# Attention on one core: the end of phi on VectorE, row sums through PSUM, M_prev's products in four pieces, a new order

## The chip, the cores and the metric

The kernel runs on one NeuronCore of a Trainium2 chip. Its engines are TensorE (PE; its weight loads are PEld), VectorE (DVE), ScalarE (ACT), GpSimd (POOL) and SyncE (SP, which here issues loads and stores). The metric is the device time of one execution in microseconds (us); less is better. Beside the times there is the profile of one execution.

## The reference

Three stages run one after the other. The change touches the first; the other two follow from its output. Of the attention stage, for each of 4 batches and 8 heads (576 tokens of 64 values):

```python
scores = scale * np.matmul(q, k.transpose(0, 1, 3, 2))
scores = np.where(causal, -1000000000.0, scores)
scores = scores - scores.max(-1, keepdims=True)
a = np.exp(scores)
a /= a.sum(-1, keepdims=True) + 1e-09
local = np.matmul(a, v)
def phi(x):
    return np.where(x > 0, x, np.exp(x) - 1.0) + 1.0
q_p = phi(q)
mem_ret = np.einsum('bhsd,bhde->bhse', q_p, M_prev)
mem_norm = np.einsum('bhsd,bhd->bhs', q_p, z_prev)[..., None] + 1e-06
g = 1.0 / (1.0 + np.exp(-beta))[None, :, None, None]
return g * (mem_ret / mem_norm) + (1 - g) * local
```

Then a mixture of experts takes each of the 2304 tokens (512 values) to one of 8 experts, picked by the largest of `x @ w_gate`, through two weight matrices with a ReLU between, and scales by the gate's probability. Last, an MLP (512 to 2048 to 512, with an ELU) works on all tokens.

## The kernel before

The attention stage goes over 16 *pairs*: a batch `b` and two neighbouring heads, pair `p = 4 b + hp`. For each pair, q and k are turned (transposed) on PE (`L92`) and copied out of PSUM into `ab`, k by DVE (`L596`) and q by ACT (`L593`). There are five blocks of scores, `i` = 3, 4, 2, 1, 0 in the code's list; block `i` < 4 holds 128 query rows and 128 (i+1) keys of both heads, block 4 the last 64 rows. Each block is a product on PE (`L639`, `L643` for the mask; `L650`, `L653` for block 4), a minimum over the row on DVE (`L661`; the scores are held negated), and an exponential on ACT (`L666`), which also sums the row into `st`. PE turns the weights (`L92` again, tile `a`), ACT or DVE copies them out (`L524` on ACT, `L527` on DVE, into `aA` for blocks 0 to 2 and `aB` for 3 and 4), and PE multiplies them with v (`L741`). The result is copied to `xT` by ACT (`L524`), and `L536` with `iw` brings it back to tokens together with the gate's logits. DVE scales it by the reciprocal row sums (`L773`, tile `ls`).

phi(q) is min(exp(q), 1) + relu(q): ACT makes both terms (`L606`, `L610`), POOL takes the minimum and adds (`L621`, `L622`, tiles `ex` and `qpT`). `L536` with `mb` multiplies it by M_prev, with w_gate already multiplied in (below), and DVE scales that (`L717`, `L721`, `L725`, tile `ms`). POOL adds `ms` and `ls` into the rows of the batch (`L785`, three adds a pair; DVE does it for the last pair).

The row sums sit in `st`, 12 to 20. Block 4's need the other half of the partitions, so PE moves them (`L739` with `swap`, into column 1000 of the PSUM tile of `L741`), DVE copies that back (`L748`), adds 1e-9 and multiplies by 1 - g (`L752`), and takes the reciprocal (`L756`).

Before pair 0, `constants` multiplies M_prev by w_gate: PE turns M_prev by halves (`L351`, four pieces), ACT copies them (`L355`), PE multiplies (`L364`, one piece for each half, 16 products each; `L365` brings z_prev), DVE copies into `mb` (`L369`, `L370`). After every fourth pair, `gate_plan` picks the experts of the batch's tokens on DVE (`L820` to `L862`), makes five pairs of one-hot tables (`L870`, `L873`, then `L885`), and PE multiplies these (`L892`). The gate of batch 3 lies in the next stage. At the end of the attention stage `first_parts` turns (`L1141`) and splits (`L1155`, `L1158`, `L1161`, tiles `x`) the first tile of tokens for the experts.

All four PSUM rings of this stage are one: four tiles of two banks (`pat`), handed out in the order of the plan.

What sets the order is a planner. Each step is an operation with an engine (or several to choose from), a cost in ns, and the keys that it reads and writes. `Plan.order` places them one by one: it takes the engine that can start soonest, and on it the step of least `prio` among those that can start within `slack` (`sa` in `KNOBS`) of the first. `off` holds the offsets of `prio`, `es` the engines that a copy may choose from. The instructions are issued in the planned order, so each engine runs its list front to back and waits at its head.

Of the kernel before, what the change touches and what calls it, by code (L numbers as in the profile page):

```python
# [94 lines left out]
class Plan:  # L95
# [169 lines left out]
def constants(tc, ctx, c, M_prev, z_prev, beta, w_gate):  # L265
# [78 lines left out]
    for h in range(2):  # L344
        for n in range(2):
            def mk(h, n):
                bk = Slot(c.rs)

                def f():
                    for x in range(8):  # L350
                        nc.tensor.transpose(bk.t[0:D, x * D:(x + 1) * D], c.mb[hss[h], 8 * n + x, 0:D], c.ident[hss[h], hss[h]])  # L351
                pl.op("PE", 450, f, r=["mld"], w=[bk], prio=K["mem"] - 30)

                def f():
                    nc.scalar.copy(mT[:, h, 8 * n:8 * n + 8, :].rearrange("p x d -> p (x d)"), bk.t[0:D, 0:512])  # L355
                pl.op("ACT", ca(512), f, r=[bk], w=[("mT", h, n)], prio=K["mem"] - 30)
            mk(h, n)
    for h in range(2):
        def mk(h):
            bq = Slot(c.rs)  # L360

            def f():
                for x in range(NPAIR):
                    nc.tensor.matmul(bq.t[hss[h], x * E:(x + 1) * E], mT[:, h, x, :], wg[:, 2 * (x % (H // 2)) + h, :], start=True, stop=True)  # L364
                nc.tensor.matmul(bq.t[hss[h], 256:256 + B * H], zr, c.ident[0:B * H, 0:B * H], start=True, stop=True)  # L365
            pl.op("PE", 900, f, r=["mld", ("mT", h, 0), ("mT", h, 1), ("raw", 0, 0), ("raw", 0, 1)], w=[bq], prio=K["mem"] - 20, dense=0.15)

            def f():
                nc.vector.tensor_copy(c.mb[hss[h], :, D:XB], bq.t[hss[h], 0:NPAIR * E].rearrange("p (x e) -> p x e", e=E))  # L369
                nc.vector.tensor_copy(c.mb[hss[h], :, XB:MW].rearrange("p x o -> p (x o)"),  # L370
                                      bq.t[hss[h], 256:256 + B * H].rearrange("p (x h) -> p x h", h=2)[:, :, h])
            pl.op("DVE", 400, f, r=[bq], w=["mb"], prio=K["mem"] - 20)
        mk(h)
# [100 lines left out]
def cps(n):  # L474
    return 330 + 0.83 * n
# [6 lines left out]
def attention(tc, ctx, c, q, k, v, M_prev):  # L482
# [55 lines left out]
    def pair(p):  # L538
# [80 lines left out]
        def f():  # L619
# [3 lines left out]
        pl.op("POOL", cps(S) + cpt(S), f, r=[se], w=[sqT, (se, "phi")], prio=at("phi"))  # L623
# [6 lines left out]
        def scores(i, ps):  # L630
# [23 lines left out]
            pl.op("PE", n / 0.6 + 90 if i < 4 else 1000, f if i < 4 else f4, r=fk, w=[s, (sa[i], "own"), (ss, "own", i)], prio=ps + O["S"], mode=1 if i < 4 else 3)  # L654
# [7 lines left out]
            pl.op("DVE", cv(2 * nn), f, r=[s], w=[(ss, "n", i)], prio=ps + O["min"])  # L662
            for h in range(2 if i < 4 else 1):
                def mk(h):
                    def f():
                        nc.scalar.activation(sa[i].t[:, h, :] if i < 4 else sa[4].t[:, 0:S].rearrange("p (y n) -> p y n", y=2), src()[:, h, :] if i < 4 else src(), AF.Exp,  # L666
                                             bias=ss.t[:, 2 * i + h:2 * i + h + 1], scale=-1.0, accum_out=ss.t[:, 12 + 2 * i + h:13 + 2 * i + h])
                    pl.op("ACT", ca(nn if i < 4 else S, acc=True), f, r=[s, (ss, "n", i)], w=[(sa[i], h), (ss, "s", i, h)], prio=ps + O["exp"] + K["hd"] * h)
                mk(h)

        def weights(i, ps):
# [10 lines left out]
            pl.op("PE", nb * 2 * TURN, f, r=[(sa[i], h) for h in range(2 if i < 4 else 1)], w=[w, (so, "own", i)], prio=ps + O["T"], mode=1)  # L682
# [9 lines left out]
            evac(f"T{i}", nb * P, dst, src, r=[w], w=[(so, i)], prio=ps + O["Te"])  # L692

        for o, i in enumerate(ORD):
            scores(i, pr + K["step"] * o)
        for o, i in enumerate(ORD):
            weights(i, pr + K["step"] * o)
# [33 lines left out]
        for g, (so, tiles, n, n0) in enumerate(((sA, (0, 1, 2), 384, P), (sB, (3, 4), 192, 512))):  # L731
            for j in range(tiles[-1] + 1):
                def mm(g, so, tiles, n, n0, j):
# [8 lines left out]
                    pl.op("PE", (n - o) / 0.6 + (60 if first else 5), f, r=[svi] + [(so, i) for i in tiles if j <= i] + ([(ss, "s", 4, 0), "swap"] if first else []),  # L742
                          w=[wx, (sx, "own", g, j)], prio=at("av") + g, mode=2)
# [66 lines left out]
def gate_plan(tc, c, b, lg, xrow, rl, rx, ring, pr):  # L810
# [4 lines left out]
    def bc(x):  # L815
# [4 lines left out]
        (330, lambda: v.tensor_reduce(G.L, lg.t.rearrange("p i c e -> p i e c"), axis=AX.X, op=ALU.add)),  # L820
# [47 lines left out]
    def table(i):  # L868
# [5 lines left out]
        pl.op("DVE", 160, f, r=[("rq", b)], w=[("rone", i)], prio=pr)  # L874
        pl.op("DVE", 170, f2, r=[("rq", b)], w=[("qone", i)], prio=pr)
# [10 lines left out]
    pl.op("DVE", 240, f, r=[("rone", i) for i in range(NI)], w=["rrow"], prio=pr)  # L886
# [839 lines left out]
```

## Time and profile before

| | |
|---|---|
| median of 3 runs | 940.1 us (939.83 to 941.58) |
| the profiled execution | 943.06 us |
| its span, first to last instruction | 941.3 us |
| mean granted TensorE clock | 0.988 of full speed |
| attention stage | to 231.5 us, where the experts' first product starts |

The profiled execution's time is 1.8 us above its span, and 3.0 us above the median. The stages of the experts and of the MLP take the other 710 us.

### The profile page before, as it was taken

Reading aid. Unit: us, or ns where it says so; the run is one execution under the profiler, and the core shown is the slowest. Engines: PE = TensorE matmul, PEld = TensorE weight load, DVE = VectorE, ACT = ScalarE, POOL = GpSimd, SP = SyncE. Lnnn points to the kernel's source line nnn. Section 1 sums busy time; section 2 is a strip of 40 time slices with the busy share of each in tenths; the row PEclk is TensorE's granted clock in tenths of the full one; section 3 lists DMA queues with packets and bytes.
Section 4 is the critical chain, followed back from the end, with each engine's and each line's share of the span. In section 5 each row is a group of like instructions: output and inputs, shape, how many; then the busy total and the mean of one; then the engine's idle time right before and its main releaser. Section 6 shows DMA issues by size and latency. Waiting matters only on the chain. (4 is left out here: it accounts for less than half of the span.)

```text
span 941.3 us, 19282 instructions
## 1 busy us (share of the span) xinstructions
PE 906.4 (96%) x7334; PEld 743.4 (79%) x7334; DVE 606.9 (64%) x1104; ACT 447.7 (48%) x879; POOL 174.7 (19%) x208
## 2 busy tenths in 40 slices
PE   9998989988999999999999899999999999999996
PEld 6676767766788888888878789988888888888895
DVE  2768686866864579548887785555565556555553
ACT  3887878876553467347676561221222122212311
POOL 2443434433101222221211100010001000100100
PEclk7999999999999999999999999999999999999998
DMA  6333343351814795589995550110011000100000
GB/s 113 83 87 103 78 128 71 82 189 59 319 35 158 256 353 194 177 280 365 329 344 194 172 184 1 34 45 1 1 46 46 1 23 12 46 1 1 23 23 23
DMA packets 97113, 110.07 MB, mean 117 GB/s; under 512 B 65391, under 2 KB 65391, under 8 KB 94705
## 3 DMA queue, kind: packets, MB, share of 16 engines
q1 hardware_dynamic: 90992, 95.26, 31.7%
q0 software_dynamic: 4800, 13.18, 3.9%
q8 instruction: 59, 0.97, 0.4%
q10 hardware_dynamic: 1216, 0.30, 0.2%
q14 instruction: 46, 0.37, 0.1%
HBM read 87.94 MB, written 23.41 MB: 118 GB/s over the span
## 5 line engine op out<-in xcount | busy, mean ns | idle before, releaser
L1535 ACT ACTIVATE elu<-pt 128x512 f32<-128x512 f32 x72 | 43.0, 598 | 266.0 <-PE pt L1527 264.0
L1560 PE MATMUL pt<-w,gh 128*128 128x512 f32 x432 | 134.2, 392 | 0.5 <-DVE gh L1439 0.5
L1327 PE MATMUL pm<-w,hh 128*128 128x512 f32 x368 | 125.1, 401 | 0.8 <-ACT y L1340 0.8
L1543 DVE TENSOR_SCALAR elu<-elu 128x512 f32<-128x512 f32 x72 | 30.8, 428 | 126.3 <-ACT elu L1535 126.3
L661 DVE TENSOR_REDUCE st<-pat 128x2 f32<-128x256 f32 (+4 forms) x80 | 62.6, 793 | 50.1 <-PE pat L643 47.9
L1560 PEld LDWEIGHTS pt<-w,gh 128*128 128x128 f32 x432 | 79.6, 188 | 16.4 <-DVE gh L1439 0.9
L666 ACT ACTIVATE a<-pat,st 128x128 f32<-128x128 f32 (+2 forms) x144 | 78.0, 547 | 25.9 <-DVE st L661 25.0
L1560 PE MATMUL pt<-w,gl 128*128 128x512 f32 x216 | 84.2, 390 | 0.0
L1327 PEld LDWEIGHTS pm<-w,hh 128*128 128x128 f32 x368 | 69.2, 188 | 14.5 <-ACT y L1340 1.2
L1327 PE MATMUL pm<-w,hl 128*128 128x512 f32 x184 | 71.9, 391 | 0.3 <-DVE hl L1161 0.3
L1527 PE MATMUL pt<-yTh,w 128*128 128x256 f32 (+1 forms) x288 | 69.2, 319 | 0.0
L639 PE MATMUL pat<-ab 64*128 64x128 f32 (+3 forms) x256 | 50.5, 492 | 7.2 <-DVE st L661 7.0
L1547 DVE SCALAR_TENSOR_TENSOR tnh<-tnh,elu 128x512 f32<-128x512 f32 x72 | 49.7, 691 | 8.4 <-ACT tnh L1539 2.4
L1284 PE MATMUL pm<-w,x 128*128 128x512 f32 x216 | 51.8, 392 | 1.2 <-DVE w L1161 0.9
L1442 DVE TENSOR_TENSOR gl<-tnh,gh 128x512 fp32r<-128x512 f32 x72 | 49.7, 691 | 4.5 <-DVE gh L1439 0.5
L1527 PEld LDWEIGHTS pt<-yTh,w 128*128 128x128 f32 x288 | 49.2, 190 | 3.9
L1551 DVE SCALAR_TENSOR_TENSOR tnh<-pt,tnh 128x512 f32<-128x512 f32 x72 | 49.6, 691 | 3.3
L1284 PEld LDWEIGHTS pm<-w,x 128*128 128x128 f32 x216 | 40.2, 188 | 10.1 <-DVE w L1161 1.4
L1161 DVE TENSOR_TENSOR hl<-pm,hh 128x512 fp32r<-128x512 f32 x46 | 31.4, 685 | 25.5 <-ACTq L1258 14.4
L1560 PEld LDWEIGHTS pt<-w,gl 128*128 128x128 f32 x216 | 40.5, 188 | 9.0 <-DVE gl L1442 0.4
L621 POOL TENSOR_SCALAR ex<-ex 128x576 f32<-128x576 f32 x16 | 34.2, 2135 | 68.2 <-ACT ex L606 68.2
L1527 PE MATMUL pt<-yTl,w 128*128 128x256 f32 (+1 forms) x144 | 45.8, 318 | 0.0
(335 smaller groups left out, 2038.5 us busy)
## 6 DMA issues: line engine op xcount, KB each, us to landing
wraw<-in_moe_w_dram SPq DMA_DIRECT2D x24, 1024.0 KB
wrbw<-in_moe_w_dram SPq DMA_DIRECT2D x12, 1024.0 KB
wide<-in_moe_w_in_dram SPq DMA_DIRECT2D x16, 512.0 KB
wf<-half SPq DMA_DIRECT2D x32, 256.0 KB
wide<-in_moe_w_out_dram SPq DMA_DIRECT2D x16, 512.0 KB
wide<-wf SPq DMA_DIRECT2D x9, 512.0 KB
v<-in_v_dram SPq DMA_DIRECT2D x32, 128.0 KB
wraw<-yd SPq DMA_DIRECT2D x14, 258.0 KB
```

The source lines that it names most:

```text
L621: nc.gpsimd.tensor_scalar(e, e, 1.0, 0.0, op0=ALU.min, op1=ALU.add)
L639: nc.tensor.matmul(s.t[:, 512 * h:512 * h + n], row(1)[hs, i * P:(i + 1) * P], row(0)[hs, 0:n], start=True, stop=False)
L661: nc.vector.tensor_reduce(ss.t[:, 2 * i:2 * i + (2 if i < 4 else 1)], src(), axis=AX.X if i < 4 else AX.XY, op=ALU.min)
L666: nc.scalar.activation(sa[i].t[:, h, :] if i < 4 else sa[4].t[:, 0:S].rearrange("p (y n) -> p y n", y=2), src()[:, h, :] if i < 4 else src ...
L1284: nc.tensor.matmul(g[hf].t, a.t[:, cc, :], b[:, 512 * hf:512 * (hf + 1)], start=(cc == 0 and n == 0), stop=(cc == 3 and n == 2))
L1327: nc.tensor.matmul(y.t, a.t[:, 2 * (q % 2) + jj, :], b[:, 512 * jj:512 * (jj + 1)], start=(q == 0 and jj == 0 and n == 0), stop=(q == 3 an ...
L1442: nc.vector.tensor_sub(lo(), src(), hi().bitcast(F32))
L1527: nc.tensor.matmul(h.t[:, n * j + n0:n * j + n1], w(cc, a, ft), b(cc), start=(cc == 0 and x == 0), stop=(cc == 3 and x == 2))
L1535: nc.scalar.activation(se.t, h.t, AF.Exp)
L1547: nc.vector.scalar_tensor_tensor(st.t, st.t, 0.0, se.t, op0=ALU.min, op1=ALU.mult)
L1551: nc.vector.scalar_tensor_tensor(st.t, h.t, 0.0, st.t, op0=ALU.max, op1=ALU.add)
L1560: nc.tensor.matmul(acc[a].t, y.t[:, n * j + P * a:n * j + P * (a + 1)], wsub(1, k, ft // 2)[:, ft % 2, :], start=(ft == 0 and x == 0), sto ...
```

## The change

- **phi.** The minimum and the addition become one DVE instruction (`fv`, L622 of the new file); the planner's table allows DVE alone (`qe`).
- **Row sums.** PE brings all ten columns of row sums into PSUM (nine through the identity, the tenth through `swap`), and DVE's addition and multiplication read them there; the copy is gone.
- **M_prev.** PE turns it in two pieces that use both halves of the array, ACT copies two tiles of twice the width, and the products are four pieces, each over both halves. DVE copies both halves at once.
- **The gate's costs** in the planner are raised (650 for 330, 195 for 160, 205 for 170, 300 for 240).
- **The table of the order** is new: an offset for each block in place of one step between blocks, other engines to choose from.

```diff
-    "m_g": -500, "wq": 0.64, "sa": 57.1, "sm": 50.0, "s2": 0.0, "step": -26642.3, "hd": -1515.1, "mem": 417833.9, "xg": 4,
+    "m_g": -500, "wq": 0.64, "sa": 70.4, "sm": 50.0, "s2": 0.0, "hd": 270570.9, "mem": -170390.9, "xg": 4,
...
+    for n in range(2):
+        def mk(n):
+            bk = Slot(c.rs)
 
             def f():
+                for x in range(8):
+                    for h in range(2):
+                        turn(nc, bk.t[0:D, 512 * h + x * D:512 * h + (x + 1) * D], c.mb[hss[h], 8 * n + x, 0:D], c.ident, h)
+            pl.op("PE", 16 * TURN, f, r=["mld"], w=[bk], prio=K["mem"] - 30, mode=1, dense=0.25)
...
+    bq = Slot(c.rs)
+    for n in range(4):
+        def mk(n):
+            def f():
+                for x in range(4 * n, 4 * n + 4):
+                    for h in range(2):
+                        nc.tensor.matmul(bq.t[hss[h], x * E:(x + 1) * E], mT[:, h, x, :], wg[:, 2 * (x % (H // 2)) + h, :], start=True, stop=True)
...
-        def f():
+        def fv():
+            nc.vector.scalar_tensor_tensor(sqT.t[:, 0:S], se.t[:, 0:S], 1.0, sqT.t[:, 0:S], op0=ALU.min, op1=ALU.add)
+
+        def fp():
             e = se.t[:, 0:S]
-            nc.gpsimd.tensor_scalar(e, e, 1.0, 0.0, op0=ALU.min, op1=ALU.add)
+            nc.gpsimd.tensor_scalar(e, e, 1.0, None, op0=ALU.min)
...
-                            nc.tensor.matmul(wx.t[h * D:(h + 1) * D, 1000:1001], c.swap[:, h * D:(h + 1) * D], ss.t[:, 20:21], start=True, stop=True)
+                            nc.tensor.matmul(wx.t[h * D:(h + 1) * D, 1000:1009], c.ident[:, h * D:(h + 1) * D], ss.t[:, 12:21], start=True, stop=True)
+                            nc.tensor.matmul(wx.t[h * D:(h + 1) * D, 1009:1010], c.swap[:, h * D:(h + 1) * D], ss.t[:, 20:21], start=True, stop=True)
...
-            nc.vector.tensor_copy(ss.t[:, 21:22], wx.t[:, 1000:1001])
+            nc.vector.scalar_tensor_tensor(ss.t[:, 12:22].rearrange("p (i h) -> p i h", h=2), wx.t[:, 1000:1010].rearrange("p (i h) -> p i h", h=2), 1.0e-9,
+                                           c.omg[:, h0:h0 + 2].unsqueeze(1).to_broadcast([P, NI, 2]), op0=ALU.add, op1=ALU.mult)
```

In the new file the lines are 2 to 8 higher: `L593` is now L595, `L661` L667, `L666` L672, `L596` L598, `L524` and `L527` L526 and L529, `L752` L755, `L773` L777, `L870` L874, `L873` L877. The lists of the expert and MLP stages hold the same instructions in the same order on every engine.

**The start, on ACT.** Before: four copies of M_prev's turned halves, then q of pair 0 (`ab`), phi's two terms and the first exponentials (`a`).

```order
L355 ACT_TABLE_LOAD
L355 COPY wraw_75<-pat_96 64x512
L355 COPY wraw_75<-pat_94 64x512
L355 COPY wraw_75<-pat_97 64x512
L355 COPY wraw_75<-pat_95 64x512
L593 ACTIVATE ab_198<-pat_97 128x576
L606 ACTIVATE ex<-pat_97 128x576
L610 ACTIVATE qpT_220<-pat_97 128x576
L666 ACTIVATE a_204,st_228<-pat_96,st_228 128x128 x2
```

Now, on the same engine, up to the first copies of turned weights (`aA`):

```order
L608 ACTIVATE ex<-pat_94 128x576
L612 ACTIVATE qpT_220<-pat_94 128x576
L672 ACTIVATE a_204,st_228<-pat_97,st_228 128x128 x2
L672 ACTIVATE a_206,st_228<-pat_96,st_228 128x256 x2
L355 COPY wraw_75<-pat_97 64x2x512
L355 COPY wraw_75<-pat_96 64x2x512
L672 ACTIVATE a_208,st_228<-pat_95,st_228 128x384 x2
L672 ACTIVATE a_210,st_228<-pat_94,st_228 128x512 x2
L672 ACTIVATE a_212,st_228<-pat_97,st_228 128x576
L336 ACTIVATE omg<-g 128x8
L337 ACTIVATE g<-g 128x8
L526 COPY aA_216<-pat_95 128x2x128
```

M_prev's copies moved from ahead of pair 0's first exponentials to between them, and the two steps that wait for beta (`L336`, `L337`) from behind two copies of weights to ahead of the first. On PE, M_prev's work moved in the same way: its products stood before the first scores, and now stand behind the scores of block 4. On SP, q and v of pair 0 are now issued ahead of M_prev, which came first; the 24 loads ahead of beta (`L325`) are the same 24.

**A gate, on DVE.** Before, between k's copy of pair 5 (`L596`) and its first minimum (`L661`), behind other steps of the gate:

```order
L596 TENSOR_SCALAR ab_198<-pat_96 128x576
L838 RECIPROCAL raw_69<-gsm_157 128x3
L907 TENSOR_REDUCE gcnt_155<-goh_154 128x8
L839 RECIPROCAL raw_70<-gsm_157 128x2
L856 TENSOR_TENSOR geq_152<-pat_97,ebase 128x40
L857 TENSOR_TENSOR geq_152<-geq_152,goh_154 128x40
L858 TENSOR_REDUCE gsl_158<-geq_152 128x5
L859 TENSOR_TENSOR gsli_159<-gsl_158,inval 128x5
```

Now `L856` (new L860) stands a pair later, among the last steps of pair 5; the tables follow it, and end ahead of pair 6's phi (L622) and first minimum:

```order
L727 RECIPROCAL rn_233<-rn_233 128x10
L860 TENSOR_TENSOR geq_152<-pat_97,ebase 128x40
L731 TENSOR_TENSOR ms_235<-pat_95,rn_233 128x2x5x72
L861 TENSOR_TENSOR geq_152<-geq_152,goh_154 128x40
L862 TENSOR_REDUCE gsl_158<-geq_152 128x5
L863 TENSOR_TENSOR gsli_159<-gsl_158,inval 128x5
L864 TENSOR_SCALAR gsli_159<-gsli_159 128x5
L865 TENSOR_SCALAR gsli_159<-gsli_159 128x5
L866 CAST grq_160<-gsli_159 128x10
L529 COPY aB_219<-pat_95 128x2x5x64
L874 TENSOR_SCALAR raw_70<-col,grq_160 128x128
L877 TENSOR_SCALAR qone<-col,grq_160 128x144
```

So the gate's DVE work, which stood between two pairs in one piece, now stands in two pieces a pair apart.

**A plain pair, on ACT.** Pair 2's last exponentials and copies before:

```order
L666 ACTIVATE a_210,st_228<-pat_97,st_228 128x512 x2
L666 ACTIVATE a_212,st_228<-pat_95,st_228 128x576
L524 COPY aA_216<-pat_97 128x4x128
L524 COPY aA_216<-pat_96 128x6x128
L524 COPY aB_218<-pat_97 128x2x5x64
L524 COPY aB_218<-pat_94 128x8x128
```

Now:

```order
L672 ACTIVATE a_210,st_228<-pat_97,st_228 128x512 x2
L526 COPY aA_216<-pat_96 128x2x128
L672 ACTIVATE a_212,st_228<-pat_94,st_228 128x576
L526 COPY aA_216<-pat_97 128x4x128
L526 COPY aB_218<-pat_94 128x2x5x64
L526 COPY aB_218<-pat_95 128x8x128
```

Block 0's small copy came from DVE to ACT, ahead of block 4's exponential; block 2's copy (128x6x128) went to DVE. In other pairs DVE takes block 1's or block 4's copy in its place. On PE, k of the next pair, which was turned between blocks 2 and 4, is now turned behind block 3.

## Rows read from the trace of the kernel before

**Rows 1.** The page, part 1: busy time, share of the span, instructions.

```profile
PE 906.4 (96%) x7334; PEld 743.4 (79%) x7334; DVE 606.9 (64%) x1104; ACT 447.7 (48%) x879; POOL 174.7 (19%) x208
```

**Rows 2.** Windows of a pair: length; busy PE, PEld, DVE, ACT, POOL; clock; DMA share; GB/s.

```profile
106.82:118.88 12.06, 11.85 (x230) 8.75 (x226) 7.91 (x14) 10.17 (x28) 5.53 (x5) 1.00 0.33 76
...
131.72:146.78 15.06, 12.74 (x252) 9.85 (x250) 12.44 (x31) 12.04 (x33) 5.54 (x5) 1.00 0.49 139
...
183.75:200.87 17.12, 14.56 (x259) 11.40 (x255) 13.77 (x41) 12.00 (x33) 5.54 (x5) 0.90 0.35 106
```

**Rows 3.** phi's exponential, once a pair: first and last start; pair 2's start.

```profile
L606 ACT ACTIVATE ex<-pat x16: 645/670/697, 13.7 to 214.1; 128x576 f32<-128x576 f32 x16
...
41.12 0.65 ACT L606 ACTIVATE ex<-pat 128x576 f32<-128x576 f32 x1
```

**Rows 4.** Waits of PE, 108.95 to 121.01 us (total, times, longest).

```profile
PE pat L92 <- ACT a L666: 0.2, 1, 0.2
```

**Rows 5.** Timeline of PE in a plain pair.

```profile
108.95 0.49 PE L639 MATMUL pat<-ab 64*128 64x128 f32 x4
...
118.03 1.51 PE L741 MATMUL pat<-aA,v 128*64 128x384 f32 x12
119.38 0.23 PE L739 MATMUL pat<-st,swap 128*64 128x1 f32 x4
```

**Rows 6.** Timeline of DVE in that pair.

```profile
109.63 0.42 DVE L661 TENSOR_REDUCE st<-pat 128x2 f32<-128x256 f32 x1 [3.97 <-PE pat L643]
...
110.16 1.07 DVE L752 SCALAR_TENSOR_TENSOR st<-st,omg 128x10 f32<-128x10 f32 x1
111.14 0.68 DVE L661 TENSOR_REDUCE st<-pat 128x2 f32<-128x512 f32 x1
```

**Rows 7.** Timeline of PE: M_prev's turns, pairs 0 and 1's first scores, pair 0's M_prev.

```profile
7.54 1.78 PE L351 MATMUL pat<-ident,mb 64*64 64x64 f32 x32
...
16.89 0.80 PE L639 MATMUL pat<-ab 64*128 64x128 f32 x4
...
22.94 0.83 PE L536 MATMUL pat<-mb,qpT 64*64 64x73 f32 x36
...
30.67 0.49 PE L639 MATMUL pat<-ab 64*128 64x128 f32 x4
```

**Rows 8.** Timeline of pair 0: beta's load, its first user, pair 1's phi.

```profile
18.84 0.60 SPq L325 DMA_DIRECT2D g<-in_beta_dram  x1
...
24.60 1.01 DVE L331 COPY iw<-ident 64x64 f32<-64x64 f32 x8
...
28.41 0.66 ACT L606 ACTIVATE ex<-pat 128x576 f32<-128x576 f32 x1
```

**Rows 9.** Timeline of DVE in the second gate.

```profile
134.69 1.49 DVE L873 TENSOR_SCALAR qone<-col,grq 128x144 bf16<-128x144 f32 x1
136.10 0.28 DVE L870 TENSOR_SCALAR raw<-col,grq 128x128 bf16<-128x128 f32 x1
...
136.50 0.28 DVE L870 TENSOR_SCALAR raw<-col,grq 128x128 bf16<-128x128 f32 x1
```

**Rows 10.** Timeline of DVE in pair 14, while POOL is idle.

```profile
205.18 0.17 DVE L752 SCALAR_TENSOR_TENSOR st<-st,omg 128x10 f32<-128x10 f32 x1
```

**Rows 11.** The page, part 5: a DVE instruction with two inputs from SBUF.

```profile
L1547 DVE SCALAR_TENSOR_TENSOR tnh<-tnh,elu 128x512 f32<-128x512 f32 x72 | 49.7, 691 | 8.4 <-ACT tnh L1539 2.4
```

**Rows 12.** Timeline of POOL in that pair.

```profile
109.80 1.40 POOL L622 TENSOR_TENSOR qpT<-ex,qpT 128x576 f32<-128x576 f32 x1
114.78 2.00 POOL L785 TENSOR_TENSOR raw<-ms,ls 128x80 f32<-128x80 f32 x3 [3.59 <-DVE ls L773]
```

**Rows 13.** Timeline of PE and DVE at the end of the stage.

```profile
222.69 0.72 PE L1141 MATMUL pat<-ident,ex 128*128 128x128 f32 x4 [0.36 <-DVE st L661]
...
224.87 0.68 DVE L1161 TENSOR_TENSOR x<-pat,x 128x512 fp32r<-128x512 f32 x1
...
231.51 1.20 PE L1284 MATMUL pm<-wq,x 128*128 128x512 f32 x4 [0.87 <-DVE ls L773]
```

More of the change, by code (lines that the diff above doesn't have):

```diff
@@ L244 @@
-    "es": {"x": ("ACT",), "T0": ("ACT", "DVE"), "T3": ("ACT", "DVE"), "k": ("DVE",), "T1": ("ACT",), "T4": ("ACT", "DVE"), "q": ("ACT",), "T2": ("ACT",)},
-    "wait": 25, "first": 34686.5, "stick": 1430924.2,
+    "nv": 2, "na": 2, "na4": 2, "nx": 2, "nls": 2, "wide": 1, "de": ("DVE", "POOL"), "busy": [0, 0, 0], "early": 120578.4, "late": 500, "mld": -2631.6,
+    "gate": 345828.7, "warm": [52, 0.0, 200.0], "qe": ("DVE",),
+    "off": {"tk": 898454.0, "tq": 882278.5, "hk": -760325.6, "hq": -759364.9, "px": 735151.8, "phi": 1087364.4, "S3": -529669.6, "S4": -1296033.8, "S2": -790035.1, "S1": -972813.3, "S0": -1302605.5, "min3": -50550.3, "min4": -410935.5, "min2": 719181.7, "min1": -45115.7, "min0": 332677.3, "exp3": 329358.7, "exp4": 631684.7, "exp2": -50550.0, "exp1": 518666.4, "exp0": 344677.0, "T3": 859665.0, "T4": 626578.9, "T2": 622423.5, "T1": 518666.8, "T0": 516520.2, "Te3": -47668.1, "Te4": 807182.8, "Te2": -1296012.9, "Te1": -509705.8, "Te0": -561958.2, "fin": -50955.8, "mm": 807201.2, "md": -1303158.8, "ms": 238704.4, "avA": -328031.8, "avB": -684654.8, "ave": -328185.5, "rw": -1410391.2, "ls": -829501.3, "add": -8135.8},
@@ L246 @@
+    "es": {"x": ("ACT",), "T0": ("ACT",), "T3": ("ACT",), "k": ("ACT", "DVE"), "T1": ("ACT", "DVE"), "T4": ("ACT", "DVE"), "q": ("ACT", "DVE"), "T2": ("ACT", "DVE")},
+    "wait": 25, "first": 1087370.1, "stick": 1227967.1,
 }
@@ L368, in f @@
             def f():
[L369 to L373, printed above, removed]
+                nc.scalar.copy(mT[:, :, 8 * n:8 * n + 8, :], bk.t[0:D].rearrange("p (h x d) -> p h x d", h=2, d=D))
@@ L374, in constants, with f @@
+    def f():
+        nc.vector.tensor_copy(c.mb[:, :, D:XB], bq.t[:, 0:NPAIR * E].rearrange("p (x e) -> p x e", e=E))
+        for h in range(2):
+            nc.vector.tensor_copy(c.mb[hss[h], :, XB:MW].rearrange("p x o -> p (x o)"),
+                                  bq.t[hss[h], 256:256 + B * H].rearrange("p (x h) -> p x h", h=2)[:, :, h])
+    pl.op("DVE", 400, f, r=[bq], w=["mb"], prio=K["mem"] - 20)
     routing_constants(tc, c)
@@ L681, in weights @@
             so = sA if i < 3 else sB
-            pl.op("PE", nb * 2 * TURN, f, r=[(sa[i], h) for h in range(2 if i < 4 else 1)], w=[w, (so, "own", i)], prio=ps + O["T"], mode=1)
+            pl.op("PE", nb * 2 * TURN, f, r=[(sa[i], h) for h in range(2 if i < 4 else 1)], w=[w, (so, "own", i)], prio=at(f"T{i}"), mode=1)
             def dst():
@@ L691, in src @@
                 return w.t.rearrange("p (z x) -> p z x", z=2)[:, :, 0:nb * D].rearrange("p z (y q) -> p z y q" if i == 4 else "p z (y q) -> p y z q", q=D)
[L692 to L697, printed above, removed]
+            evac(f"T{i}", nb * P, dst, src, r=[w], w=[(so, i)], prio=at(f"Te{i}"))
+        for i in ORD:
+            scores(i)
+        for i in ORD:
+            weights(i)
         sx, srn = Slot(r_xT), Slot(r_rn)
@@ L885, in f @@
         v.tensor_scalar(c.rrow, c.rone, c.row, None, op0=ALU.mult)
-    pl.op("DVE", 240, f, r=[("rone", i) for i in range(NI)], w=["rrow"], prio=pr)
+    pl.op("DVE", 300, f, r=[("rone", i) for i in range(NI)], w=["rrow"], prio=pr)
     def f():
```

58 lines of the change are left out of this document (20 added, 38 removed).

## The prediction

> **What bounds it now.** I read the engines' busy shares first: TensorE 96% [rows 1]. That share is a mean over three stages, and two of them (experts, MLP) hold the same instructions in the same order before and now, so I let them shift as a block. Everything is decided ahead of the experts' first product.
>
> In that stage I took the windows between one pair's first scores and the next's [rows 2]. A plain pair lasts 12.06 us with TensorE busy 11.85, ACT 10.17, DVE 7.91; the two with a gate last 15.06 and 17.12. How much all gates cost comes from phi's exponential, once a pair: from 41.12 (pair 2) to 214.1 (pair 15) are 13 intervals, 172.95 us [rows 3]; 13 plain ones would be 156.8. The excess is **16.2 us**, and it lies at the three gates, which are what can be won in the middle of the stage.
>
> In the wait view of a plain pair TensorE waits 0.2 us [rows 4], and its timeline runs from the first scores (108.95) to the products with v (118.03) without a hole that anything else could fill [rows 5]. So a plain pair is bound by the list on TensorE itself; ACT is next, with 1.9 us of room; DVE has a hole of 3.97 us ahead of its first minimum [rows 6]. POOL works 5.53 of 12.06 and nobody on the path waits for it. The start is the other place to look at: pair 0's first scores come at 16.89 only, behind M_prev's work [rows 7].
>
> **The start.** M_prev's turns begin at 7.54, when its load has landed [rows 7]. q and k of pair 0 are now issued ahead of it, and nothing stands between them and the first scores. They land by 7.5 at best and by 8.7 if the constant work ahead of them fills the time; I take 8.7. Eighteen turns at 1.78/32 us each [rows 7] are 1.0, and a copy of 576 columns is 0.7 (phi's exponential has the same width, [rows 3]). First scores at 10.4: 6.5 us earlier than 16.89.
>
> Most of this is lost at beta. Its load is issued at 18.84, and the first instruction that needs it starts at 24.60 [rows 8], so it lands between 19.4 (the issue's end) and 24.6. The same 24 loads still stand ahead of it. Its two steps on ACT now stand ahead of all copies of turned weights, so pair 0, which would be done earlier, waits for beta there. I take 21.0, near the lower third, since its first user is itself late in DVE's list. Then: 0.4 for the two steps, an estimate from L752's 0.17 for a step as small; four copies on ACT of 256, 512, 768 and 1024 columns, 2560 in all, at phi's 0.65 per 576 = 2.9, of which the turns hide none; then phi's exponential to pair 1's first scores as before, 30.67 - 28.41 = 2.3 [rows 7, 8]. That is 26.5, against 30.67: -4.2. Against it, pair 0's product with M_prev (0.83, [rows 7]) and its scaling leave pair 0 and lie in pair 1: +1.2 with the part of the scaling that doesn't hide. **Start: -3.0** (at beta 24.6 and the rest as above +0.6; at beta 19.4 -4.6, -5 with the scaling hidden).
>
> **The gates.** Before, the gate's DVE work stands in one piece between k's copy and the first minimum; now it stands in two, a pair apart. Is each shorter than the hole of 3.97 us [rows 6]? The second piece: five pairs of tables at 0.40, the spacing of two L870 with an L873 between them [rows 9], are 2.0; the table of rows 0.4; eight small steps at 0.17 to 0.2 (a step of that size is L752 undisturbed, [rows 10]) 1.6; phi 0.8 (0.69 for 512 columns from two SBUF inputs, [rows 11], times 576/512); and 0.5 for the wider copy that DVE now has. Together 5.3, which is 1.3 beyond the hole. The first piece, some fifteen small steps at 0.2 and a reduction over 320 columns (0.42 for 256, 0.68 for 512, [rows 6]), is about 3.6 and fits, but pushes k's copy back, by at most its own length: +0.7. TensorE's own part of a gate stays: 12.74 busy against 11.85 [rows 2], +0.9. That makes 2.9 a gate, 8.7 for three, and I keep 1.5 for the third one, whose window shows a clock of 0.90 and two us more than the second [rows 2]. 10.2 instead of 16.2: **-6.0**. The bounds: both pieces spill and pull ACT along, -1; each fits, -10. One part of it is nearly sure: L873 took 1.49 us where POOL's minimum ran, against the 0.40 that an undisturbed pair of tables takes [rows 9], and phi is no longer on POOL; that alone is over 1 us a gate.
>
> **Plain pairs: phi.** 0.8 us on DVE, in the hole of 3.97, ahead of the first minimum and free as long as the exponentials of phi come before it. Without that cover it would be 0.8 a pair. POOL loses 3.5 us a pair, which nobody waited for.
>
> **Plain pairs: row sums.** The addition with the gate's factor took 1.07 us in a plain pair [rows 6], while POOL's addition for phi ran (109.80 to 111.20, [rows 12]), and 0.17 at 205.18 with POOL idle [rows 10]. So the second minimum, now at 111.14, can start 0.7 earlier, and ACT's exponential behind it too. On TensorE this gives nothing, since its list is full; it is worth 0 to 0.4. TensorE pays: two small products with 9 columns more, against 0.23 for the four records of the old ones [rows 5]; +0.1. A rule bears on the first of these numbers: the Trainium skill (SBUF — State Buffer, Who interferes with whom) says that DVE's second read port is GpSimd's, under an exclusive lock, so that a DVE instruction with two SBUF inputs stands still while GpSimd reads. The trace agrees (1.07 against 0.17), and by it the new form, with one input in PSUM, would not stretch. By the same rule phi on DVE, with two SBUF inputs, could stand behind POOL's adds; that is a rival below.
>
> **Plain pairs: order.** Block 0's copy stands ahead of block 4's exponential on ACT, and k is turned behind block 3. Block 4's weights can be turned later by the copy's length, but the copy of block 2, the longest, left ACT, so ACT has as much work as before. I let the nine plain pairs lose the 0.1 of the row sums: **+0.9** (from -5, the second minimum's gain in each of 13, to +4).
>
> **The end.** Turning the experts' first tokens (0.72 on TensorE, hidden in a wait) and splitting them (0.68 on DVE) [rows 13] now stand ahead of the last `ls`, for which the first expert product waits (its idle 0.87 ends with `ls`). **+0.7** (0 to 1.5).
>
> Sum: -3.0 - 6.0 + 0.9 + 0.7 = **-7.4**. The profiled execution, 943.06 us, becomes 935.7; the median of the runs was 940.1, 3.0 lower, so the prediction is **932.7**.
>
> **Rivals.** *More than that* (0.18): beta lands at 19.4 and the gates fit, start -5, gates -9, the rest +0.3: 926.4. For it: DVE's hole is nearly as long as the second piece. Against it: twenty-odd small steps on DVE have never filled a hole without a spill in this trace.
>
> *No change* (0.10): beta lands at 24.6, the start gives +0.6, the gates only the 3 us of L873's stalls, with +0.9 and +0.7: -0.8, 939.3. For it: nothing in the trace shows beta landing before 24.6.
>
> *Slower* (0.13): in each plain pair block 4's exponential waits behind block 0's copy, which itself waits for a turn on TensorE; TensorE then has nothing to turn before its products with v. The price is at most the copy and one hop, 1.0 us. It decides the sign from (3.0 + 6.0 - 0.7)/13 = 0.64 us a pair; at 1.0, 13 - 8.3 = +4.7: 944.8. For it: ACT has only 1.9 us of room in 12.06 [rows 2]. Against it: the wait would have to come in every pair, and DVE's minima come earlier.
>
> *phi behind POOL's adds* (0.03): the three adds of 2.00 us end at 116.8 in the pair [rows 12], and phi would meet half of them at the worst, 1.0; in 15 pairs 15 - 8.3 gives 946.8. Against it: phi's place is ahead of the next first minimum, 109.63 + 12.06 = 121.7, over 3 us after their end. The section of the Trainium skill named above is what would make it a stall.
>
> **The numbers.** The forecast holds 0.56, 929.5 to 937 by itself. For 8 in 10 the range takes in most of the larger gain and the whole of no change: **925.5 to 941**. 0.2%, some 1.9 us, is about what a measurement of this kernel can tell from no change. Faster: 0.56 + 0.18 and a little of the third = 0.75; same 0.10; slower 0.15 (the last two rivals, less the part of the first of them that stays under 0.64).
>
> **What would show it.** Pair 1's first scores at 26 to 27 us, with ACT waiting for beta's load ahead of its first copies of weights: the start. Windows of 13 to 14 us where a gate's pieces stand, and no L877 over 0.5 us: the gates. Plain windows of 12.0 to 12.3 and L755 at 0.17: plain pairs; anything over 12.5, with TensorE waiting for ACT's `a` ahead of block 4's turns, and the prediction is wrong towards slower. First expert product at 224: the sum. It is wrong as well if beta lands late, if DVE's pieces hold up ACT behind the first minimum, or if the granted clock, 1.00 in plain windows [rows 2], falls where TensorE now waits.

## The result, and the profile after

The changed kernel takes **925.46 us** (median of 4 runs, 924.92 to 926.61), the kernel before 939.97 (939.39 to 941.58). The ratio is 0.9845, 95% interval 0.9828 to 0.9862: 14.5 us faster. The forecast was 932.7, 7.4 us faster, with a range from 925.5, so the measured time lies just under the range and the gain is about twice the forecast one. The rival *more than that* had 926.4, in part for other reasons: the gates gave nearly what it wanted, the start did not, and most of the missing gain came in the plain pairs (those that no gate touches), where I had written +0.9.

The page of the changed kernel, its part 1, as [rows 1]:

```profile
PE 894.0 (97%) x7404; PEld 739.9 (80%) x7404; DVE 611.6 (66%) x1105; ACT 444.0 (48%) x875; POOL 117.7 (13%) x176
```

TensorE has 12 us less of busy time although it has 70 instructions more; POOL lost a third of its work. Where it went, from phi's exponential once a pair, as [rows 3] (first and last start; pair 2's start):

```profile
L608 ACT ACTIVATE ex<-pat x16: 633/658/671, 9.8 to 196.1; 128x576 f32<-128x576 f32 x16
...
37.08 0.66 ACT L608 ACTIVATE ex<-pat 128x576 f32<-128x576 f32 x1
```

Pair 2 starts at 37.08 instead of 41.12, and from pair 2 to pair 15 are 159.0 us instead of 172.95. The windows of [rows 2] run from one pair's phi exponential to the next, not from first scores to first scores as the prediction has it; in the plain pairs of the kernel before the two distances are alike. Three windows of the changed kernel (length; busy PE, PEld, DVE, ACT, POOL; clock): a plain pair from first scores to first scores, and two, between exponentials, in which a gate's second piece stands.

```profile
100.42:112.07 11.65, 11.42 (x234) 8.91 (x231) 8.50 (x14) 9.98 (x26) 2.01 (x3) 1.00 0.24 54
84.57:97.98 13.41, 12.61 (x254) 9.99 (x252) 11.35 (x24) 11.54 (x32) 3.69 (x5) 1.00 0.41 93
182.46:196.12 13.66, 12.59 (x256) 10.21 (x254) 12.52 (x29) 11.08 (x32) 3.66 (x5) 1.00 0.65 221
```

The plain pair went from 12.06 to 11.65 (from first scores to first scores, seven plain pairs take 11.65 to 11.67), and the clock of the third gate's window from 0.90 to 1.00. Between phi's exponentials the changed kernel's plain pairs alternate (11.43, 11.81), because ACT does that step at another place in the pair; this is no measure of the period. The sum on DVE, and the timeline of TensorE in that plain pair, as [rows 6, 5], with the first scores, block 4's products (L656), the first turns and the products with v:

```profile
101.37 0.16 DVE L755 SCALAR_TENSOR_TENSOR st<-pat,omg 128x10 f32<-128x10 f32 x1
```

```profile
100.42 0.49 PE L645 MATMUL pat<-ab 64*128 64x128 f32 x4
...
104.04 1.13 PE L656 MATMUL pat<-ab 64*64 64x288 f32 x7
...
105.81 2.56 PE L92 MATMUL pat<-ident,a 64*128 64x64 f32 x50
...
108.93 1.52 PE L748 MATMUL pat<-aA,v 128*64 128x384 f32 x12
...
112.07 0.49 PE L645 MATMUL pat<-ab 64*128 64x128 f32 x4
```

From the first scores to the products with v are 8.51 us now, 9.08 before [rows 5]. From there to the next first scores are 3.14; without the small products it is 2.98 (phi_alone and new_sums_old, below), so 0.16 is the price of the row sums on TensorE.

The start on TensorE and ACT, as [rows 7, 8], of the changed kernel:

```profile
9.90 0.49 PE L645 MATMUL pat<-ab 64*128 64x128 f32 x4
...
20.64 0.21 ACT L336 ACTIVATE omg<-g 128x8 f32<-128x8 f32 x1 [2.15 <-DMA g<-in_beta_dram]
...
27.59 0.49 PE L645 MATMUL pat<-ab 64*128 64x128 f32 x4
```

First scores at 9.90 (forecast 10.4), beta landed at 20.6 (forecast 21.0), pair 1's first scores at 27.59 (forecast 26.5). The end, as [rows 13]:

```profile
213.42 0.93 PE L1288 MATMUL pm<-wq,x 128*128 128x512 f32 x3 [1.40 <-DVE raw L789]
```

### The profile page after: what moved, and what is told of

It is laid out like the page before. It is cut to its first block, busy times and chain, and to the rows that moved or that the text cites. A ratio compares the mean times of both kernels' runs of the same rounds, so it can differ in the third digit from the quotient of the medians.

```text
span 923.7 us, 19288 instructions
## 1 busy us (share of the span) xinstructions
PE 894.0 (97%) x7404; PEld 739.9 (80%) x7404; DVE 611.6 (66%) x1105; ACT 444.0 (48%) x875; POOL 117.7 (13%) x176
## 5 line engine op out<-in xcount | busy, mean ns | idle before, releaser
L672 ACT ACTIVATE a<-pat,st 128x128 f32<-128x128 f32 (+2 forms) x144 | 78.2, 548 | 8.1 <-DVE st L667 5.0
L667 DVE TENSOR_REDUCE st<-pat 128x2 f32<-128x256 f32 (+4 forms) x80 | 63.7, 798 | 18.8 <-PE pat L649 14.7
L645 PE MATMUL pat<-ab 64*128 64x128 f32 (+3 forms) x256 | 46.9, 474 | 2.1 <-ACT ab L595 2.1
L789 POOL TENSOR_TENSOR raw<-ms,ls 128x80 f32<-128x80 f32 (+2 forms) x45 | 30.2, 696 | 141.9 <-DVE ls L777 128.1
```

The lines of the kernel that those rows point to most:

```text
L645: nc.tensor.matmul(s.t[:, 512 * h:512 * h + n], row(1)[hs, i * P:(i + 1) * P], row(0)[hs, 0:n], start=True, stop=False)
L667: nc.vector.tensor_reduce(ss.t[:, 2 * i:2 * i + (2 if i < 4 else 1)], src(), axis=AX.X if i < 4 else AX.XY, op=ALU.min)
```

## The experiments

Each experiment starts from one of the two kernels with its planned order written out and replayed, so that an edit moves nothing but what the edit itself names. Two theories are told apart. Theory P: phi on POOL held up DVE's sum (the addition and multiplication of the row sums, L752, in the new file L755), and through it TensorE, in every plain pair. Theory O: the new order shortened the plain pairs. Three chips ran the kernels; the kernel before took 941.1 to 942.7 us there (medians of 9 to 17 runs), so that differences of 1 or 2 us between runs of different chips are read from the traces and not from the times. phi_alone, sums_alone, order_alone and new_sums_old ran on one chip, long_sums_psum and mprev_first on another, the rest on the third. "Pairs 2 to 15" is the distance from pair 2's phi exponential to pair 15's; periods of plain pairs are from first scores to first scores.

**before_again.** No edit: the kernel before, once more.

> The kernel before, its planned order written out, the same instructions in the same order on every engine: a second profile of it, to see what in the first one is that execution's alone. Expected: plain pairs 12.06 again; the first scores of pair 0 between 14 and 17 us and the stretches at half clock in the gates not in the same places; span 937 to 941.

Measured: 942.61 us, span 940.9. Its chief rows are phi's exponential once a pair (first and last), and TensorE in a plain pair:

```profile
L606 ACT ACTIVATE ex<-pat x16: 644/668/694, 12.1 to 211.9; 128x576 f32<-128x576 f32 x16
...
38.96 0.65 ACT L606 ACTIVATE ex<-pat 128x576 f32<-128x576 f32 x1
```

```profile
106.81 0.49 PE L639 MATMUL pat<-ab 64*128 64x128 f32 x4
...
109.96 0.85 PE L536 MATMUL pat<-iw,xT 64*64 64x72 f32 x40
...
110.86 1.19 PE L650 MATMUL pat<-ab 64*64 64x288 f32 x8
...
112.85 0.34 PE L92 MATMUL pat<-ident,a 64*128 64x64 f32 x4
...
115.89 1.52 PE L741 MATMUL pat<-aA,v 128*64 128x384 f32 x12
...
118.86 0.49 PE L639 MATMUL pat<-ab 64*128 64x128 f32 x4
```

From pair 2 on it is the first profile again: 211.94 - 38.96 = 172.98 against 172.95. Ahead of pair 2 it is 2.16 us earlier (38.96 against 41.12): that much of the first profile's start belonged to that execution alone. TensorE's clock stood at half in the start of both, to 21.1 us there and to 19.0 here. My guess that the half-clock stretches move was wrong; they come at the same two gates:

```profile
84.00:88.00 4.00, 4.00 (x94) 3.02 (x90) 2.59 (x3) 2.52 (x8) 1.42 (x3) 0.59 0.34 77
190.00:194.00 4.00, 4.00 (x94) 3.03 (x91) 2.77 (x3) 2.28 (x8) 1.70 (x3) 0.62 0.10 21
```

So the start gained 38.96 - 37.08 = 1.9 us against this execution, 4.0 against the first, and the sum to the experts' first product is -15.9 or -18.1 (229.29 and 231.51 against 213.42); the medians differ by 14.5.

**phi_alone.** The kernel before, phi's two POOL instructions replaced:

```diff
-            nc.gpsimd.tensor_scalar(e, e, 1.0, 0.0, op0=ALU.min, op1=ALU.add)
-            nc.gpsimd.tensor_tensor(sqT.t[:, 0:S], e, sqT.t[:, 0:S], op=ALU.add)
-        pl.op("POOL", cps(S) + cpt(S), f,
+            nc.vector.scalar_tensor_tensor(sqT.t[:, 0:S], se.t[:, 0:S], 1.0, sqT.t[:, 0:S], op0=ALU.min, op1=ALU.add)
+        pl.op("DVE", cv(S), f,
```

> The kernel before, its order kept step for step; only phi's end moves from POOL to one DVE instruction, placed ahead of the pair's first minimum. Theory P (POOL's phi held up DVE's small additions and tables, which two SBUF inputs or a shared port explain, and this delayed the exponentials and so TensorE a little in every pair): the addition L752 at about 0.17 instead of 1.07, plain pairs 11.5 to 11.7 instead of 12.06, no L873 over 0.5 us, 6 to 10 us faster than before. Theory O (the new table of the order is what shortens the plain pairs): plain pairs stay at 12.0 to 12.1, only the gates gain some 3 us.

Measured: 931.38 us, ratio 0.9886 (0.9855 to 0.9917), 11.3 us faster, more than the 6 to 10 expected (the runs lie from 927.86 to 936.19, the profiled one at 928.49). DVE and TensorE in a plain pair (11.60 us from first scores to first scores):

```profile
103.85 0.17 DVE L752 SCALAR_TENSOR_TENSOR st<-st,omg 128x10 f32<-128x10 f32 x1
```

```profile
102.71 0.49 PE L639 MATMUL pat<-ab 64*128 64x128 f32 x4
...
105.79 0.86 PE L536 MATMUL pat<-iw,xT 64*64 64x72 f32 x40
...
106.47 1.13 PE L650 MATMUL pat<-ab 64*64 64x288 f32 x7
...
111.33 1.52 PE L741 MATMUL pat<-aA,v 128*64 128x384 f32 x12
...
114.31 0.49 PE L639 MATMUL pat<-ab 64*128 64x128 f32 x4
```

Theory P holds in its mechanism: the addition at 0.17, plain pairs at 11.6, every L873 at 0.29; pairs 2 to 15 last 162.5 instead of 173.0. Theory O, that only the new table shortens a plain pair, falls. phi's own 0.76 us on DVE lies in the hole ahead of the first minimum, as forecast.

**sums_alone.** The kernel before, only the row sums changed, as in the diff above (nine columns through the identity; the copy's step left empty).

> The kernel before, its order kept; only the row sums go through PSUM, phi stays on POOL. Theory P in the form that only the addition's stall matters: plain pairs 11.65 to 11.8 (0.16 of them for the small products), L752 at 0.17, the gates' tables still stalled, 3 to 5 us faster. Theory O: plain pairs 12.1 to 12.2, 1 to 2 us slower.

Measured: 940.18 us, ratio 0.9975 (0.9959 to 0.9992), 2.5 us faster, a little under what was expected. The sum on DVE, and TensorE:

```profile
107.17 0.16 DVE L752 SCALAR_TENSOR_TENSOR st<-pat,omg 128x10 f32<-128x10 f32 x1
```

```profile
106.14 0.49 PE L639 MATMUL pat<-ab 64*128 64x128 f32 x4
...
109.97 1.13 PE L650 MATMUL pat<-ab 64*64 64x288 f32 x7
...
117.99 0.38 PE L639 MATMUL pat<-ab 64*128 64x128 f32 x2
```

This run moves the stall and the copy of 0.15 ahead of it (in new_sums_old, below, that copy is back and costs nothing that shows); phi is still on POOL. Block 4's products stand 3.83 us behind the first scores where before_again has 4.05, and the pair is 11.85, although 0.16 was paid for the small products. So the stall held 0.4 us of every plain pair. The gates' tables stay stalled (one L873 still at 1.49).

**order_alone.** The changed kernel with phi on POOL and the row sums as they were:

```diff
-    "gate": 345828.7, "warm": [52, 0.0, 200.0], "qe": ("DVE",),
+    "gate": 345828.7, "warm": [52, 0.0, 200.0], "qe": ("POOL",),
...
-            nc.vector.scalar_tensor_tensor(ss.t[:, 12:22].rearrange("p (i h) -> p i h", h=2), wx.t[:, 1000:1010].rearrange("p (i h) -> p i h", h=2), 1.0e-9,
+            nc.vector.tensor_copy(ss.t[:, 21:22], wx.t[:, 1000:1001]); nc.vector.scalar_tensor_tensor(ss.t[:, 12:22].rearrange("p (i h) -> p i h", h=2), ss.t[:, 12:22].rearrange("p (i h) -> p i h", h=2), 1.0e-9,
```

> The changed kernel with its order and its M_prev kept, but phi back on POOL and the row sums back to one moved column and the sum from SBUF. Theory P: the stall of the addition is back (about 1 us), plain pairs 11.9 to 12.1, tables stalled in the gates, 932 to 936. Theory O: plain pairs 11.4 to 11.5 (0.16 less than now, without the small products), 923 to 927.

Measured: 925.54 us, as fast as the whole change; theory P had 932 to 936. By itself that speaks for theory O, but it has a flaw: the changed file's form of phi on POOL is shorter (a minimum alone), and the sum takes 0.22 to 0.55 us in its plain pairs, not 1.07. The next run takes that away. (The kernel before with this shorter minimum in its old order was not run.)

**order_long.** order_alone with POOL's minimum as in the kernel before:

```diff
-            nc.gpsimd.tensor_scalar(e, e, 1.0, None, op0=ALU.min)
+            nc.gpsimd.tensor_scalar(e, e, 1.0, 0.0, op0=ALU.min, op1=ALU.add)
```

> As order_alone, but POOL's minimum in the form of the kernel before (a minimum and an addition of zero, 2.14 us where order_alone had 1.65). Theory P (what counts is where phi on POOL lies against the sum): the sum's stall grows from 0.2 to 0.55 to about 1.0 and the second minimum with it, plain pairs 11.7 to 11.9, 928 to 930. Theory O (the new order has room for the stall): plain pairs 11.45 to 11.6 and 925 to 926 as order_alone.

Measured: 930.18 us, ratio 0.9877 (0.9855 to 0.9899). POOL, then DVE, ACT and TensorE in a plain pair (12.20):

```profile
100.71 2.13 POOL L626 TENSOR_SCALAR ex<-ex 128x576 f32<-128x576 f32 x1 [3.21 <-ACT ex L608]
102.92 1.40 POOL L627 TENSOR_TENSOR qpT<-ex,qpT 128x576 f32<-128x576 f32 x1
```

```profile
103.31 1.04 DVE L755 SCALAR_TENSOR_TENSOR st<-st,omg 128x10 f32<-128x10 f32 x1
...
105.24 0.47 ACT L672 ACTIVATE a<-pat,st 128x256 f32<-128x256 f32 x1 [1.13 <-DVE st L667]
...
106.31 1.19 PE L656 MATMUL pat<-ab 64*64 64x288 f32 x8 [0.34 <-ACT a L672]
...
114.37 0.49 PE L645 MATMUL pat<-ab 64*128 64x128 f32 x4
```

The sum lasts until POOL's addition ends (104.3), ACT stands idle for 1.13 us ahead of block 1's exponentials, and block 4's products, which need the PSUM tile that these exponentials read, start 4.14 us behind the first scores (102.17 to 106.31; 3.62 in the changed kernel). A half microsecond of POOL's time costs 5.6 us in pairs 2 to 15 (158.7 in order_alone, 164.3 here), 4.6 between the medians. The new order has no room for the stall. In these two runs the period of a plain pair goes with the length of its sum: about 11.5 where the sum takes 0.22, 11.7 at 0.51 to 0.55, 11.95 at 0.70, 12.2 at 1.04. The plain pairs here are 11.68 to 12.20, 11.99 on average, where 11.7 to 11.9 was expected: hardly shorter than the 12.06 of the kernel before.

**long_sums_psum.** order_long with the row sums through PSUM again, phi on POOL in the long form.

> order_long with the row sums through PSUM as in the changed kernel; phi stays on POOL in the long form. Theory P (the sum's two SBUF inputs meet POOL's phi, and its stall is what the plain pairs lose): the sum takes 0.15, plain pairs 11.92 - 0.49 + 0.16 = 11.4 to 11.6, and 926 to 927.5, 3 to 4 us less than order_long, with the gates still stalled. Rival (POOL's phi is itself late for TensorE, or holds other things up): plain pairs stay at 11.9 or above and the time at 930 or more.

Measured: 927.22 us (923.81 to 928.11), plain pairs 11.65 to 11.69, the sum

```profile
102.40 0.16 DVE L755 SCALAR_TENSOR_TENSOR st<-pat,omg 128x10 f32<-128x10 f32 x1
```

while POOL's phi runs (its addition from 102.03 to 103.43). As theory P wanted: the sum's second SBUF input makes the stall; POOL's phi in itself is not late for TensorE. With phi on POOL in its long form, the plain pairs are those of the changed kernel: once the row sums go through PSUM, phi's move adds nothing to them.

**new_sums_old.** The changed kernel, phi on DVE, the row sums back to SBUF (second half of order_alone's diff).

> The changed kernel, order kept; only the row sums go back to one moved column, copy and sum from SBUF, phi stays on DVE. Theory P: with POOL out of the way the sum from SBUF does not stall (0.17), TensorE saves the 0.16 of the small products in each of 16 pairs: 922.5 to 924, plain pairs 11.3 to 11.65. Rival (the sum through PSUM is needed also with phi on DVE): the addition stalls behind POOL's three adds and the time is 926 or more.

Measured: 923.76 us (922.82 to 924.58), 1.7 less than the changed kernel; plain pairs 11.48 to 11.51, 0.16 to 0.17 less each; the sum takes 0.17.

```profile
99.78 0.49 PE L645 MATMUL pat<-ab 64*128 64x128 f32 x4
...
111.26 0.49 PE L645 MATMUL pat<-ab 64*128 64x128 f32 x4
```

With phi off POOL nothing is left for the row sums' new way to win, and its products cost what they take.

**mprev_first.** The changed kernel with M_prev's load, turns, copies, products and copy put ahead of all of pair 0 in the written order; no code changed.

> The changed kernel, order kept, but M_prev's load, turns, copies, four pieces of products and copy stand ahead of everything of pair 0, as in the kernel before. My forecast's view (ACT waits for beta at 20.6 whatever pair 0 does before): first scores at 12 to 14 instead of 9.9, pair 1's first scores at 27.6 to 28.5, 925.5 to 926.5. Rival (M_prev's place is what the start gained): pair 1's first scores at 29.5 or later, 927.5 or more.

Measured: 926.45 us (925.91 to 927.18). TensorE's first scores of pairs 0 and 1:

```profile
14.99 0.80 PE L645 MATMUL pat<-ab 64*128 64x128 f32 x4
...
28.81 0.49 PE L645 MATMUL pat<-ab 64*128 64x128 f32 x4
```

Five microseconds in the first scores are 1.2 in pair 1's and about 1 in the time: most of what the first scores gain is lost further on. Pair 1's first scores are a little later than the 27.6 to 28.5 expected, since ACT reached beta's steps at 22.0 only and did not wait there.

**beta_early.** The changed kernel; in the written order of SP the three loads that end with beta's (L324, L325) stand right behind M_prev's (L319), ahead of pair 1's.

> The changed kernel, order kept; only the three loads of the gate's weights and of beta go ahead of pair 1's 11 loads on SP. If ACT's wait of 2.15 us for beta bounds the start: pair 1's first scores at about 25.5 instead of 27.6, 922.5 to 924. Rival: pair 1's q and k or pair 0's v now land 2 us later and the start waits for those instead: within 0.2%.

Measured: 920.55 us, ratio 0.9776 (0.9758 to 0.9794), 4.9 less than the changed kernel, twice what was expected.

```profile
10.27 0.60 SPq L325 DMA_DIRECT2D g<-in_beta_dram  x1
```

```profile
16.98 0.21 ACT L336 ACTIVATE omg<-g 128x8 f32<-128x8 f32 x1
...
22.65 0.49 PE L645 MATMUL pat<-ab 64*128 64x128 f32 x4
```

ACT waits no more. From pair 0's first scores to pair 1's are 14.1 us (8.51 to 22.65) instead of 17.7: 3.6, of which 2.15 were the wait. The rest, 1.4, fits the clock, though no run takes the clock apart from the wait. In the changed kernel TensorE stood nearly idle for 2.4 us and then was granted half of its clock (windows of the changed kernel, columns as in [rows 2]):

```profile
19.00:21.40 2.40, 0.14 (x6) 0.00 (x2) 0.25 (x2) 0.72 (x4) 0.00 (x0) 1.00 0.34 73
21.40:25.00 3.60, 3.59 (x48) 3.01 (x50) 1.58 (x2) 3.04 (x5) 0.00 (x0) 0.53 0.46 103
```

In beta_early the clock is 1.00 through the same work (it falls to half once later, at the third gate, from 175.7 to 179.1). The last 1.4 us are first scores that come at 8.51 there, and at 8.7 to 9.9 in the other runs with this start.

**beta_early_sums_old.** Both together.

> new_sums_old and beta_early together. If both gains are on TensorE's list and independent: 920.5 to 922.5, faster than either alone. If they share the same slack: as new_sums_old, 923 to 924.

Measured: **919.69 us** (917.97 to 920.77), ratio 0.9770 (0.9752 to 0.9789), the fastest version, a little under the 920.5 to 922.5 expected: 5.8 below the changed kernel, 22 below the kernel before on that chip. Against beta_early it is 0.9, less than the 1.7 of new_sums_old but not to be told from it: the runs spread over 2.8 us.

## Why the prediction was wrong, step by step

**Plain pairs: the failed step.** It reads: "On TensorE this gives nothing, since its list is full; it is worth 0 to 0.4." The list was not full. The period of the plain pairs went from 12.06 to 11.66, -5.2 over 13 intervals, where the forecast had +0.9. The prediction had the chain in its bounds ("-5, the second minimum's gain in each of 13") and put it at nothing. Working the runs together: the end of the sum's stall gave -0.46 (12.06 to 11.60, phi_alone), the order without the stall -0.11 (11.60 to 11.49, new_sums_old), the small products +0.17 (11.49 to 11.66, the changed kernel); that is the -0.40 measured. The profile forecast from has the sign in it already: in its pair 2 the sum starts (45.15) when POOL's addition is nearly done (45.47) and takes 0.35, not 1.07, and that pair lasts 11.66 (first scores at 43.94 and 55.60) where the other plain ones last 12.06.

```profile
45.15 0.35 DVE L752 SCALAR_TENSOR_TENSOR st<-st,omg 128x10 f32<-128x10 f32 x1
```

```profile
43.94 0.49 PE L639 MATMUL pat<-ab 64*128 64x128 f32 x4
...
55.60 0.49 PE L639 MATMUL pat<-ab 64*128 64x128 f32 x4
```

What I misread is the wait view. It showed 0.2 us for TensorE [rows 4], and busy time of 11.85 in 12.06 [rows 2]; without the stall the same work is done in 0.46 less, and TensorE's busy time in the pair falls with it, from 11.83 (before_again) to 11.45 (phi_alone). A wait of the block 4 products was there in the kernel before, but the records of neighbouring matmuls overlap, and a wait up to the length of that overlap leaves hardly any idle time. In before_again the products with `iw` (L536) begin at 109.96, their row ends at 110.81, and block 4's products begin at 110.86: 0.05 of idle time. In phi_alone the row is as long (0.86), but block 4's products begin 0.18 ahead of its end. From start to start it is 0.90 and 0.68, with the same 40 products between. Another 0.22 lies between block 4's products and the first turns behind them (1.99 and 1.77); what makes that part is open. The Trainium skill (Perfetto Trace Analysis, the note ahead of its first section) says that for judging how close a kernel is to roofline, matmul busy time is a bad metric, because matmuls are pipelined; this case agrees, with 0.4 us of 11.83 that went away with the same work. What shows such waits is the distance between the starts of neighbouring groups in two pairs or two kernels. And the chain was to be read forward: I followed the stall to the second minimum and to ACT's exponentials, and stopped. The next step is the tile those exponentials read, which block 4's products write. In the changed kernel's order, too, this is the point that decides (order_long).

**Start: -3.0.** Right in its mechanism (first scores, wait for beta, pair 1) and within 1.1 us at each station. Measured -4.0 against the profile forecast from, -1.9 against the second one. The other traces say that even this is much: pair 2's exponential starts at 38.7 to 39.0 in three of the four profiles with the old start (41.12 is the exception), and at 37.1 to 38.8 in the five with the new start and beta's load in its place, so that against those three the start gives some 1 us on average. The prediction's last sign, a clock that falls where TensorE now waits, did come there: half of full for 3.4 us in the changed kernel (0.53 above), for 7 to 10 us in the other four. That M_prev's place is worth little as long as beta is late was shown by mprev_first.

**Gates: -6.0.** Measured with plain pairs of 11.66: 159.04 - 13 x 11.66 = 7.5 us of excess, where 16.2 stood and 10.2 was forecast: -8.7, inside the bounds given (-1 to -10). phi off POOL alone gives -4.5 (phi_alone: 162.5 - 13 x 11.60 = 11.7). That is not the L873 stalls alone, since the half clock at gates 1 and 3 is gone in that run too; at the second gate, with full clock in both, the window between exponentials went from 15.06 to 13.75. The order alone, with the tables still behind phi on POOL, gives more (order_long: 164.3 - 13 x 11.99 = 8.4, so -7.8), and the two do not add. Which part of the order does it (the gate's costs, the table, M_prev) no run takes apart. The half clock at gates 1 and 3 is gone in the changed kernel too; I had kept 1.5 for it. One reading was wrong besides: the 1.49 us of L873 at 134.69 [rows 9] ran beside POOL's addition, not its minimum.

```profile
134.69 1.40 POOL L622 TENSOR_TENSOR qpT<-ex,qpT 128x576 f32<-128x576 f32 x1
```

One expectation failed: "no L877 over 0.5 us". In the first gate, DVE and POOL of the changed kernel:

```profile
84.97 1.69 POOL L789 TENSOR_TENSOR raw<-ms,ls 128x384 f32<-128x384 f32 x2 [4.57 <-DMA xd<-raw]
```

```profile
85.03 1.04 DVE L877 TENSOR_SCALAR qone<-col,grq 128x144 bf16<-128x144 f32 x1
```

The tables meet POOL's adds now, in all three gates (L874 at 0.94 in the second, L877 at 0.78 in the third).

**phi on DVE: nothing.** Right. Its price is hidden; the rival that it stands behind POOL's adds did not come, since it takes 0.74 to 0.76 in each of the 16 pairs.

**Row sums: +0.1.** The small products measured +0.16 to +0.17 a pair. The forecast's +0.9 for the plain pairs was made of this price alone.

**The end: +0.7.** It measured about zero: from phi's exponential of pair 15 to the experts' first product are 17.3 us now, 17.4 before. The product waits longer for its input (1.40 against 0.87, now released by the last addition), but the products with `iw` ahead of it begin 15.0 us behind that exponential now (211.16), 15.7 before (229.79).

**The sum.** From the profile forecast from to the experts' first product: -4.0 (start), -5.2 (plain pairs), -8.7 (gates), -0.1 (end), together -18.1, at 213.42 where 224 was forecast. Pairs 2 to 15 alone give 13.9 (172.95 and 159.04), beside the medians' 14.5.

**Rivals.** *Slower*, with block 4's exponential late behind block 0's copy, did not come: no plain pair is over 11.7. *No change* rested on a late beta; it landed at 20.6.

**Why both halves look alike.** phi_alone gives 11.3 us, the order with M_prev (order_long) 11.4, all together 14.5. By pairs 2 to 15, phi_alone's gain is 10.5, of which 6.0 are the plain periods' and 4.5 the gates'; order_long's is 8.7, of which 0.9 and 7.8. The two halves overlap at the gates, where the order alone takes nearly all that the whole change takes, while in plain pairs the gain is the stall's.

## What to carry to other kernels

An engine that the wait view calls full can still wait: compare the starts of its neighbouring groups between two periods, and follow a stall on another engine forward, through who reads its result and whose buffer that reader frees, until it meets the engine that sets the time. A tiny instruction with two SBUF inputs that takes six times as long as the same one elsewhere (1.07 against 0.17) is such a stall; move or shorten what runs on POOL beside it, or read one input from PSUM, but not both, since the second cure then only costs (1.7 us here). When a small load that a whole engine waits for stands far back in its queue, move it before reordering the compute that waits for it: three loads moved were worth a third as much as the whole change.

## What the runs showed of the hardware that was not expected

- On POOL, the minimum of 128x576 takes 1.65 us with one operation and 2.13 with an added zero; in the plain pairs of the new order that half microsecond decided whether the sum took 0.22 to 0.55 or 0.51 to 1.04.
- A DVE instruction with one tensor input also stalls beside POOL's additions: L877 (128x144 into bf16) took 1.04 instead of 0.28, L874 0.76. The Trainium skill (SBUF — State Buffer, Who interferes with whom) lists `tensor_scalar` among the operations that can take the ports DVE shares with GpSimd, when their operands meet its conditions; these stalls agree with it, though the trace does not show in which mode the two ran. A sum with one input in PSUM took 0.16 beside POOL's phi.
- TensorE's clock fell to half (0.50 of full, the level of 1.2 GHz) at the same two gates in two profiles of the kernel before. In the start it did so in every profile with beta's load in its old place: right behind the 2.4 us of near idleness in the changed kernel, but in order_long and long_sums_psum it was at 0.50 from 17 to 18 us already, with TensorE busy and ahead of that idle time, so that idle time is not shown to be what brings it. In the two runs with beta's load moved it stayed at 1.00 from 8 us to the end of the start.
